# Carried state times C on two 64-row halves of the array, and y kept in two banks

## The chip, the core and the metric

The kernel runs on one core of a Trainium2 chip. The core has a matrix engine (TensorE, PE in the rows of the profile, with its weight loads shown apart as PEld), a vector engine (DVE), a scalar engine (ACT), a general engine (POOL) and a queue that only issues transfers (SP). They work side by side and wait for each other through semaphores. PE writes its products to PSUM, eight banks of 128 partitions by 2 KB; DVE and ACT read them from there into the on-chip memory SBUF. The metric is the device time of one execution in microseconds. Before the change it is 125.18 us, the median of three runs (125.15 to 126.35).

## What is computed

Two stages follow each other. The first is a state-space layer (4 batches, 8 heads, 768 tokens, 32 channels per head, state size 16), given in chunks; the second is a gated feed-forward layer on its output, 3072 tokens by 256.

```python
for c in range(nc):                       # chunks; state starts at zero
    cum = np.cumsum(la, axis=-1)          # la = log a, per batch and head
    M = einsum('bhin,bhjn->bhij', Cc, Bc) * exp(cum_i - cum_j) * causal
    y_intra = einsum('bhij,bhjd->bhid', M, xc)
    y_inter = einsum('bhin,bhnd->bhid', Cc, state) * exp(cum)
    y[:, :, sl] = y_intra + y_inter
    state = exp(sum(la)) * state + sum_j(Bc x xc * exp(cum_last - cum_j))
...
gate = maximum(x @ w_gate, 0); val = x @ w_val          # x = y, 3072 x 256
out = gate * val @ w_out                                # 256 -> 1536 -> 256
```

## The kernel before, in words

**Tiling.** The kernel takes chunks of 128 tokens, six to a batch, and handles them two at a time as a pair: p runs from 0 to 11, three pairs to a batch (`PPB` is 3). Pairs 0 to 5 (batches 0 and 1) load B and C by token and transpose them on PE. Pairs 6 to 11 (`p >= NRUN`, called packed in this text) take B and C from `seqB` and `seqC`, loaded once per batch in long runs along the sequence by `load_seq`, scaled on POOL (`seq_scale`), and turned by DVE (`seq_turn`, `seq_part`). The scale factors of these come from `ah`, the decays loaded by `load_a`.

**One pair.** `G` makes C times B for eight heads: 16 matmuls that use 32 rows and 128 columns of the array each (32\*128 in the profile), into four banks. `gevac` masks the products and brings them to `gs`, on ACT (then POOL for the mask) and on DVE. `Dm` and its inner `dterm` multiply them by x: 16 matmuls of 128 rows and 32 columns (128\*32) into y. `inter` adds the carried state times C to the same y. The states S come from `astep` and `sevac` (pairs 0 to 5), or from `arun` and its `evac` (packed pairs). `yevac` copies y to `yT`, the input of the feed-forward stage. Pairs 0 and 1 have `split_y` in place of `inter`, `Dm` and `yevac`; there y already has two banks, and the `dterm` matmuls come first.

**The carried state before.** For each chunk but the first of a batch, `inter` issues two matmuls with all 128 rows and columns (128\*128), one for each half t of the heads; the stationary operand is the masked state, 128 by 128, in which a row that belongs to the other half is zero. A pair so has four such matmuls (pairs 1, 2, 4, 5, 7, 8, 10, 11) or two (pairs 0, 3, 6, 9, whose first chunk has no carried state).

**Feed-forward.** It runs in blocks of 512 tokens, b from 0 to 5. `gv` and `gvp` make gate and val in two banks, ACT applies the relu to gate (`gv_relu`), DVE multiplies it by val (`gv_mul`). `fout` then makes the output in 12 matmuls per 128 tokens, ACT copies it (`foevac`), and SP or ACT sends it off.

**Order.** The order on every engine is the order in which the program is written: `in_order` chains the instructions. `section(p, n)` writes a pair's `inter` and `Dm`, the next pair's `arun` and `G`, and the evacuations; the last loop sets a block's `gv` calls, a section, two or three `outs`, another section and the last `outs` behind each other.

**Banks.** One of the eight PSUM banks holds the running state (`A_ps`). The other seven are handed out by `bank()` to whatever product comes next, each time one whose previous product has been read. A first matmul into a bank waits until the reader of the bank's previous product is through.

Of the kernel before, what the change touches and what calls it, by code (L numbers as in the profile page):

```python
# [29 lines left out]
def kernel(  # L30
# [43 lines left out]
    st = {}  # L74
# [91 lines left out]
    smasks = const.tile([128, 2, 2, 128], BF16)  # L166
# [138 lines left out]
    def load_a(q):  # L305
        q.dma_start(out=ah, in_=a[B0:NB].rearrange("b (t q) (j u) -> (q j) (b t) u", t=2, u=U))

    def seq_start():
        for v in (a0, tot, lead):
            nc.gpsimd.memset(v, 0.0 if v is a0 else 1.0)  # L310
        nc.gpsimd.memset(smasks, 0.0)
# [100 lines left out]
    def scale_bc(p, eng):  # L412
        b, c0 = p // PPB, 2 * (p % PPB)
        s = st[p]
        if p >= NRUN:
            bs = att.tile([128, 2, 128], BF16, tag="bt", name="bt")
            for t in range(2):
                hs = slice(4 * t, 4 * t + 4)
                eng.tensor_tensor(
                    out=bs.rearrange("s i (q t n) -> s i t q n", q=4, t=2)[:, :, t],  # L420
                    in0=s["br"][:, :, hs],
                    in1=scaleBC[:, b, c0:c0 + 2, 0, hs].unsqueeze(3).to_broadcast(
                        [128, 2, 4, N]), op=ALU.mult)
            s["B"] = [bs[:, i] for i in range(2)]
            return
# [174 lines left out]
    def arun(p):  # L600

        c0 = 2 * (p % PPB)
        for c in range(max(c0 - 2, 0), c0 + 1):
            v0, v1 = (0 if c < c0 else 1), (1 if c == c0 - 2 else 2)
            pc, i = p - (p % PPB) + c // 2, c % 2
            for q in range(4):
                out = XY[32 * q:32 * q + 32, v0:v1]
                rhs = st[pc]["x"][i].rearrange("s (t q d) -> s t q d", t=2, q=4)[:, :, q]
                nc.tensor.matmul(
                    out=out, lhsT=st[pc]["B"][i][:, 32 * q:32 * q + 32],  # L610
                    rhs=rhs.unsqueeze(1).to_broadcast([128, v1 - v0, 2, 32]),
# [3 lines left out]
        n = att.tile([128, 2, 2, 128], BF16, tag="SS", name="SS", bufs=3)  # L615

        def evac():
            shape = [128, 2 * (2 - v0), 4, 32]
            nc.vector.tensor_tensor(
                out=n[:, v0:2].rearrange("p v t (q d) -> p (v t) q d", q=4),  # L620
                in0=XY[:, v0:2].rearrange("p v (t d) -> p (v t) d", t=2).unsqueeze(
                    2).to_broadcast(shape),
                in1=smasks[:, v0:2].rearrange("p v t (q d) -> p (v t) q d", q=4),
                op=ALU.mult)
            for v in range(v0, 2):
                S[2 * p + v] = n[:, v]
# [3 lines left out]
    def y_bank(s):  # L630
        if "y" not in s:
            s["y"] = bank("y", (128, 2, 2, 128))
            s["open"] = False

    def split_y(p):

        s = st[p]
        yb = [bank("y%d" % k, (128, 2, 128)) for k in range(2)]
        carried = [S.pop(2 * p + i) if 2 * (p % PPB) + i else None for i in range(2)]
        for k in (1, 0):  # L640
            for i in range(2):
                dterm(p, yb[k][:, i], k, i, i == 0)
        for i in range(2):
            for k in (1, 0):
                if carried[i] is not None:
                    nc.tensor.matmul(
                        out=yb[k][:, i], lhsT=carried[i][:, k], rhs=s["CT"][:, i],
                        start=False, stop=True, skip_group_check=True)
        dst = yT[:, :, p * 256:(p + 1) * 256].rearrange("r t (i m) -> r t i m", i=2)
        nc.vector.tensor_copy(dst[:, 1], yb[1])  # L650
        nc.scalar.copy(out=dst[:, 0], in_=yb[0])

    def inter(p, i):
# [4 lines left out]
        Sm = S.pop(2 * p + i)  # L658
        for t in range(2):
            nc.tensor.matmul(  # L660
                out=s["y"][:, t, i], lhsT=Sm[:, t], rhs=s["CT"][:, i],
                start=not s["open"], stop=False, skip_group_check=True)
            s["open"] = True

    def dterm(p, out, k, i, start):

        s = st[p]
        for c in range(4):
# [3 lines left out]
                rhs=(s["gs"][:, c, 2 * i + k] if p >= NRUN else  # L672
                     s["gs"][:, h // 2, 2 * i + h % 2]), start=start, stop=True,
                tile_position=(0, 32 * c), skip_group_check=True)

    def Dm(p):
        s = st[p]
        y_bank(s)
        for i in range(2):
            for k in range(2):  # L680
                dterm(p, s["y"][:, k, i], k, i, not s["open"] and i == 0 and k == 0)
        s["open"] = True

    def yevac(p, eng):
        s = st[p]
        dst = yT[:, :, p * 256:(p + 1) * 256]
        src = s["y"].rearrange("r t i m -> r t (i m)")
        if eng is None:
            nc.scalar.copy(out=dst[:, 0], in_=src[:, 0])
            nc.vector.tensor_copy(dst[:, 1], src[:, 1])  # L690
        elif eng is nc.scalar:
            eng.copy(out=dst, in_=src)  # L692
        else:
            eng.tensor_copy(dst, src)
# [179 lines left out]
    dall = decay()  # L874
    decay_evac(dall)
# [44 lines left out]
    load_a(nc.scalar)  # L920
    gvp(0, 1, 2)
    gvp(0, 1, 4)
# [152 lines left out]
```

## Time and profile before

| | |
|---|---|
| median of the runs | 125.18 us (125.15 to 126.35) |
| the profiled execution's own time | 124.8 us |
| its span, from the first to the last instruction | 123.0 us |
| PE busy / its weight loads | 118.3 us (96%) / 81.1 us |
| DVE, ACT, POOL busy | 92.1, 74.6, 49.7 us |
| granted clock of PE, mean | 1.000 |

The profile's rows give a line of the kernel, the engine, the operation with output and inputs, its shape and how often it ran. In the list of groups busy time and the mean of one follow the bar, then the idle time ahead of them on their engine. In a timeline the row begins with its start and its length in us, and ends with the idle time of the engine before it and what ended that. A matmul's length includes its run through the array, so two that follow each other overlap in a timeline; the pitch from start to start tells what each costs PE.

### The profile page before, as it was taken

To read this page: it belongs to the slowest core of one execution; us is meant where nothing else is said; L and a number is where in the kernel's file an instruction comes from. 1 tells how busy PE (TensorE), PEld (TensorE's weight loads), DVE (VectorE), ACT (ScalarE), POOL (GpSimd) and SP (SyncE) were. 2 spreads that over 40 slices of the span, in tenths; PEclk is the share of its full clock that TensorE was granted. 3 is DMA by queue.
4 is the path that set the end of the run, shared out by engine and by line. 5 is a ranking of instruction groups with operands and counts; after the bars stand their busy time and mean duration, and the time that the engine had idled before them with its cause. 6 is when DMAs were issued, how large, how long until landed. Compare 5 with 4: busy or idle time off the path is not lost.

```text
span 123.0 us, 3313 instructions
## 1 busy us (share of the span) xinstructions
PE 118.3 (96%) x1251; PEld 81.1 (66%) x1257; DVE 92.1 (75%) x196; ACT 74.6 (61%) x148; POOL 49.7 (40%) x102
## 2 busy tenths in 40 slices
PE   6999999999999999999999999999999999999990
PEld 4678795578888989744478644588544587444780
DVE  2786898889999859879995889981898770678420
ACT  4376668888764461767663776746676644767310
POOL 7989741885745676477330640030700030000000
PEclk9999999999999999999999999999999999999999
DMA  2999999999989979969921282003200003100022
GB/s 61 201 193 209 168 167 190 130 102 174 162 101 278 140 137 191 199 201 211 132 24 62 83 137 22 5 0 106 70 3 0 0 5 128 43 0 0 0 91 85
DMA packets 63568, 12.95 MB, mean 105 GB/s; under 512 B 55168, under 2 KB 63552, under 8 KB 63552
## 3 DMA queue, kind: packets, MB, share of 16 engines
q1 hardware_dynamic: 54160, 9.47, 42.9%
q0 software_dynamic: 4272, 2.36, 14.6%
q10 hardware_dynamic: 5120, 0.90, 3.9%
q8 instruction: 10, 0.16, 0.5%
q14 instruction: 6, 0.05, 0.1%
HBM read 11.94 MB, written 3.15 MB: 123 GB/s over the span
## 4 chain that ended last, share of the span: by engine, by line
PE 95%; DVE 1%; issue 0%; ACTq 0%; ACT 0%; DVEq 0%
PE o L760 25%; PE val L707 20%; PE gate L704 18%; PE gate L734 7%; PE val L734 6%; PE w L189 4%; PE y L670 3%; PE g L544 3%; PE y L660 2%; PE A_ps L586 1%; PE tp L486 1%; PE wdec L232 1%; PE dec L279 1%; PE o L796 1%; PE bp L463 1%; PE fdec L247 0%
## 5 line engine op out<-in xcount | busy, mean ns | idle before, releaser
L719 DVE TENSOR_TENSOR h<-r,val 128x512 bf16<-128x512 bf16 x54 | 35.9, 685 | 10.2 <-ACT r L715 9.6
L715 ACT ACTIVATE r<-gate 128x512 bf16<-128x512 f32 x54 | 32.2, 598 | 12.2 <-PE gate L704 11.7
L707 PE MATMUL val<-yT,wv 128*128 128x512 bf16 x108 | 32.1, 379 | 0.3
L760 PE MATMUL o<-wo,h 128*128 128x256 bf16 x276 | 32.3, 273 | 0.0
L704 PE MATMUL gate<-yT,wg 128*128 128x512 bf16 x102 | 30.8, 379 | 0.0
L552 POOL TENSOR_SCALAR_AFFINE_SELECT gs<-gs 128x512 bf16<-128x512 bf16 (+1 forms) x26 | 13.6, 547 | 41.6 <-ACT gs L569 41.6
L760 PEld LDWEIGHTS <-h 128*128 128x128 bf16 x276 | 26.2, 98 | 4.0
L576 DVE TENSOR_TENSOR gs<-g,maskUT 128x512 bf16<-128x512 f32 (+1 forms) x32 | 17.6, 601 | 7.1 <-PE g L544 4.0
L707 PEld LDWEIGHTS <-wv 128*128 128x128 bf16 x108 | 10.6, 98 | 12.7
L704 PEld LDWEIGHTS <-wg 128*128 128x128 bf16 x108 | 10.4, 98 | 11.1
L569 ACT CAST gs<-g 128x512 bf16<-128x512 f32 (+1 forms) x26 | 11.8, 512 | 2.9 <-PE g L544 2.9
L742 ACT ACTIVATE r<-gate 128x512 bf16<-128x512 f32 x18 | 10.6, 604 | 2.7 <-PE gate L734 2.3
L749 DVE TENSOR_TENSOR h<-r,val 128x512 bf16<-128x512 bf16 x18 | 11.8, 678 | 0.3 <-ACT r L742 0.2
L734 PE MATMUL gate<-yT,wg 128*128 128x256 bf16 x72 | 10.8, 273 | 0.0
L734 PE MATMUL val<-yT,wv 128*128 128x256 bf16 x72 | 10.8, 273 | 0.0
L779 ACT COPY ob<-o 128x512 f32<-128x512 f32 x6 | 3.5, 586 | 8.6 <-PE o L760 8.6
L774 ACT COPY ob<-o 128x256 f32<-128x256 f32 x10 | 3.7, 373 | 7.3 <-PE o L760 6.8
L734 PEld LDWEIGHTS <-wv 128*128 128x128 bf16 x72 | 7.0, 98 | 0.9
L692 ACT CAST yT<-y 128x512 bf16<-128x512 f32 x10 | 5.9, 586 | 2.4 <-PE y L670 2.3
L734 PEld LDWEIGHTS <-wg 128*128 128x128 bf16 x72 | 6.7, 98 | 0.9
L189 PE MATMUL w<-warm 128*128 128x256 bf16 x27 | 5.9, 380 | 1.2 <-DVE tmask L159 1.2
L452 POOL CAST xb<-xr 128x512 bf16<-128x512 f32 x10 | 6.1, 612 | 1.0 <-DMA xr<-in_x_dram 1.0
(124 smaller groups left out, 123.2 us busy)
## 6 DMA issues: line engine op xcount, KB each, us to landing
xr<-in_x_dram SPq DMA_DIRECT2D x24, 128.0 KB, 3.7
out_dram<-ob SPq DMA_DIRECT2D x6, 256.0 KB, 2.6
out_dram<-ob SPq DMA_DIRECT2D x9, 128.0 KB, 1.8
wo<-in_moe_w_out_dram POOLq DMA_DIRECT2D x1, 768.0 KB, 8.9
seqB<-in_B_dram SPq DMA_DIRECT2D x2, 384.0 KB, 3.7
seqC<-in_C_dram SPq DMA_DIRECT2D x2, 384.0 KB, 4.2
br<-in_B_dram SPq DMA_DIRECT2D x12, 64.0 KB, 3.2
wg<-in_moe_w_gate_dram POOLq DMA_DIRECT2D x3, 128.0 KB, 4.3
```

What stands on the lines that cost most here:

```text
L189: nc.tensor.matmul(out=w[:, 0:cols], lhsT=warm[:, 0:128], rhs=warm[:, 0:cols], start=True, stop=True)
L552: nc.gpsimd.affine_select(out=dst, in_=dst, pattern=[[0, n], [1, 128]], compare_op=ALU.is_ge, fill=0.0, base=0, channel_multiplier=-1)
L569: nc.scalar.copy(out=d[:, q, h], in_=g[q][:, h])
L576: nc.vector.tensor_tensor(out=d[:, q, h], in0=g[q][:, h], in1=m[:, h], op=ALU.mult)
L704: nc.tensor.matmul(out=g, lhsT=wg[:, k, fs], rhs=yT[:, k, tk], start=(k == 0), stop=(k == 1))
L707: nc.tensor.matmul(out=v, lhsT=wv[:, k, fs], rhs=yT[:, k, tk], start=(k == 0), stop=(k == 1))
L715: nc.scalar.activation(r, g, AF.Relu)
L719: nc.vector.tensor_tensor(out=fst[b][:, f], in0=r, in1=v, op=ALU.mult)
L734: nc.tensor.matmul(out=o[:, j], lhsT=w[:, k, fs], rhs=yT[:, k, tk], start=(k == 0), stop=(k == 1), skip_group_check=True)
L742: nc.scalar.activation(r, g, AF.Relu)
L749: nc.vector.tensor_tensor(out=fst[b][:, f:f + 2, u * 256:(u + 1) * 256], in0=r, in1=v, op=ALU.mult)
L760: nc.tensor.matmul(out=o[:, ts % 2], lhsT=fst[b][:, f, ts * 128:(ts + 1) * 128], rhs=wo[:, f], start=(f == 0), stop=(f == NF - 1), skip_gr ...
```

## The change

- `inter` and `split_y` share a new function, `carried`. For each chunk it issues two matmuls that each use 64 rows and all 128 columns of the array: half k takes rows 64k to 64k+63 of the state and of C and writes y's half k. The number of matmuls stays as it was.
- y of a pair lies in two banks, `y0` and `y1`, one for each half, instead of one bank; `yevac` reads them with two copies.
- In packed pairs the heads stand in their natural order. `load_seq` and `load_a` fetch head 2q+t instead of 4t+q: four transfers where there were two, and four where there was one. Two of `load_a`'s transfers stand earlier, ahead of `decay_evac` on ACT; the other two stand behind `gvp(0, 1, 0)` and `gvp(0, 1, 2)`.
- The packed pairs' masked state has 128 columns per chunk instead of 256; `dmask` takes the place of `smasks`, filled by two POOL copies instead of a memset and eight. `scale_bc` of a packed pair is one POOL instruction instead of two.

```diff
@@ load_seq
-            q.dma_start(
-                out=r.rearrange("p t u n -> p t (u n)"),
-                in_=src[b].rearrange("(t q) (j u) n -> (q j) t (u n)", t=2, u=U))
+            for t in range(2):
+                q.dma_start(
+                    out=r[:, t].rearrange("p u n -> p (u n)"),
+                    in_=src[b].rearrange("(q t) (j u) n -> t q j (u n)", t=2, u=U)[t])
@@ load_a
-    def load_a(q):
-        q.dma_start(out=ah, in_=a[B0:NB].rearrange("b (t q) (j u) -> (q j) (b t) u", t=2, u=U))
+    def load_a(k):
+        nc.scalar.dma_start(
+            out=ah[:, k],
+            in_=a[B0 + k // 2].rearrange("(q t) (j u) -> t q j u", t=2, u=U)[k % 2])
@@ seq_masks
-        for q in range(4):
-            r = slice(32 * q, 32 * q + 32)
-            for v in range(2):
-                nc.gpsimd.tensor_copy(
-                    smasks[r, v, :, 32 * q:32 * q + 32],
-                    tmask[r].unsqueeze(2).to_broadcast([32, 2, 32]))
+        for k in range(2):
+            r = slice(64 * k, 64 * k + 64)
+            nc.gpsimd.tensor_copy(dmask[r].rearrange("p q m -> p (q m)"), smask[r, k])
@@ scale_bc
-            for t in range(2):
-                hs = slice(4 * t, 4 * t + 4)
-                eng.tensor_tensor(
...
+            eng.tensor_tensor(
+                out=bs.rearrange("s i (h n) -> s i h n", h=NH), in0=s["br"],
...
@@ arun
-                rhs = st[pc]["x"][i].rearrange("s (t q d) -> s t q d", t=2, q=4)[:, :, q]
+                rhs = st[pc]["x"][i][:, 64 * q:64 * q + 64]
...
-            shape = [128, 2 * (2 - v0), 4, 32]
+            shape = [128, 2 - v0, 2, 64]
...
@@ y_bank, carried
-            s["y"] = bank("y", (128, 2, 2, 128))
+            s["y"] = [bank("y%d" % k, (128, 2, 128)) for k in range(2)]
...
+    def carried(p, i, start):
+
+        s = st[p]
+        Sm = S.pop(2 * p + i)
+        for k in range(2):
+            r = slice(64 * k, 64 * k + 64)
+            nc.tensor.matmul(
+                out=s["y"][k][:, i], lhsT=Sm[r] if p >= NRUN else Sm[r, k],
+                rhs=s["CT"][r, i], start=start, stop=True, tile_position=(64 * k, 0),
+                skip_group_check=True)
@@ split_y
         for i in range(2):
-            for k in (1, 0):
-                if carried[i] is not None:
-                    nc.tensor.matmul(
-                        out=yb[k][:, i], lhsT=carried[i][:, k], rhs=s["CT"][:, i],
-                        start=False, stop=True, skip_group_check=True)
+            if 2 * (p % PPB) + i:
+                carried(p, i, False)
@@ inter
-        Sm = S.pop(2 * p + i)
-        for t in range(2):
-            nc.tensor.matmul(
-                out=s["y"][:, t, i], lhsT=Sm[:, t], rhs=s["CT"][:, i],
-                start=not s["open"], stop=False, skip_group_check=True)
-            s["open"] = True
+        carried(p, i, not s["open"])
+        s["open"] = True
@@ yevac
-        dst = yT[:, :, p * 256:(p + 1) * 256]
-        src = s["y"].rearrange("r t i m -> r t (i m)")
...
+        for k in range(2):
+            dst = yT[:, k, p * 256:(p + 1) * 256]
+            src = s["y"][k].rearrange("r i m -> r (i m)")
+            if eng is nc.scalar:
+                eng.copy(out=dst, in_=src)
...
@@ the program's order
     dall = decay()
+    load_a(0)
+    load_a(1)
     decay_evac(dall)
...
     gvp(0, 1, 0)
-    load_a(nc.scalar)
+    load_a(2)
     gvp(0, 1, 2)
+    load_a(3)
     gvp(0, 1, 4)
```

Line numbers of the two kernels differ a little: L660 and L646 (the carried matmuls) become L635, L670 (`dterm`) becomes L667, L760 (`fout`) becomes L754, L544 (`G`) becomes L540.

The first place is PE at pair 7, between the output matmuls of block 2 (`o`) and the `dterm` matmuls. `SS` is the masked state. Before:

```order
L760 MATMUL o_1463<-wo_146,h_1240 128x256
L660 LDWEIGHTS SS_1400
L660 MATMUL y_1479<-CTs_1114,SS_1400 128x128
...
L670 LDWEIGHTS xb_1253
L670 MATMUL y_1479<-gs_1421,xb_1253 32x128
```

After, at the same place:

```order
L754 MATMUL o_1470<-wo_146,h_1247 128x256
L635 LDWEIGHTS SS_1406
L635 MATMUL y0_1486<-CTs_1117,SS_1406 128x128
L635 LDWEIGHTS SS_1406
L635 MATMUL y1_1487<-CTs_1117,SS_1406 128x128
...
L667 LDWEIGHTS xb_1259
L667 MATMUL y0_1486<-gs_1427,xb_1259 32x128
```

There are four carried matmuls in both, each with its load of weights (the repeats are left out); they now go to the two banks in turn.

The second place is PE in block 3, where the last matmul of `G` is followed by the first output matmul of the block (`o`), with the semaphore that it waits for. Before:

```order
L544 MATMUL g2_1720<-CTs_1598,BM_1599 128x128
L544 LDWEIGHTS BM_1599
L544 MATMUL g3_1721<-CTs_1598,BM_1599 128x128
L760 LDWEIGHTS h_1565
L760 MATMUL o_1748<-wo_146,h_1565 128x256 [waits Activation_49]
```

After:

```order
L540 MATMUL g2_1728<-CTs_1606,BM_1607 128x128
L540 LDWEIGHTS BM_1607
L540 MATMUL g3_1729<-CTs_1606,BM_1607 128x128
L754 LDWEIGHTS h_1574
L754 MATMUL o_1757<-wo_146,h_1574 128x256 [waits DVE_49]
```

No instruction moved; the bank that `o` is given did. Before, it was that of the block's last `gate`, read by ACT. Now it is that of the last `val`, read by DVE's multiply. In block 4 it is the same; in block 2 `o` is given the bank that held y0 of the same section.

The third place is ACT early in the program, between the evacuation of pair 0's `G` and that of the decay products (`scaleBC`). Before:

```order
L569 CAST gs<-g_219 128x512
L569 CAST gs<-g_220 128x512
L289 COPY scaleBC<-dec 128x3x4x8 x2
L651 CAST yT<-y_278 128x256
L512 ACTIVATE BT<-tp,tmask 128x256
```

After:

```order
L565 CAST gs<-g_219 128x512
L565 CAST gs<-g_220 128x512
L307 DMA ah<-in_a_dram 128x1x24 x2
L290 COPY scaleBC<-dec 128x3x4x8 x2
L652 CAST yT<-y_280 128x256
```

Two transfers of `ah` are issued there now.

More of the change, by code (lines that the diff above doesn't have):

```diff
@@ L614, in arun @@
         v0 = 0 if c0 else 1
-        n = att.tile([128, 2, 2, 128], BF16, tag="SS", name="SS", bufs=3)
+        n = att.tile([128, 2, 128], BF16, tag="SS", name="SS", bufs=3)
         def evac():
-            shape = [128, 2 * (2 - v0), 4, 32]
+            shape = [128, 2 - v0, 2, 64]
             nc.vector.tensor_tensor(
[L620 to L624, printed above, removed]
+                out=n[:, v0:2].rearrange("p v (q m) -> p v q m", q=2),
+                in0=XY[:, v0:2].unsqueeze(2).to_broadcast(shape),
+                in1=dmask.unsqueeze(1).to_broadcast(shape), op=ALU.mult)
             for v in range(v0, 2):
@@ L680, in Dm @@
             for k in range(2):
-                dterm(p, s["y"][:, k, i], k, i, not s["open"] and i == 0 and k == 0)
+                dterm(p, s["y"][k][:, i], k, i, not s["open"] and i == 0)
         s["open"] = True
@@ L685, in yevac @@
         s = st[p]
[L686 to L694 removed]
+        for k in range(2):
[3 more added lines that the diff above has]
+                eng.copy(out=dst, in_=src)
+            else:
+                eng.tensor_copy(dst, src)
     fst = {}
```

23 lines of the change are left out of this document (9 added, 14 removed).

## The prediction

> **What bounds the kernel now.** I read the page first: the busy times and the chain that ended last, and then who waited for whom.
>
> ```profile
> span 123.0 us, 3313 instructions
> PE 118.3 (96%) x1251; PEld 81.1 (66%) x1257; DVE 92.1 (75%) x196; ACT 74.6 (61%) x148; POOL 49.7 (40%) x102
> ...
> PE 95%; DVE 1%; issue 0%; ACTq 0%; ACT 0%; DVEq 0%
> ```
>
> ```profile
> ACT r L715 <- PE gate L704: 11.7, 44, 0.3
> ```
>
> PE is busy for 118.3 of 123.0 us and carries 95% of the chain; ACT waits for PE 44 times, not the other way. So time is won or lost only where PE's pitch from start to start changes, or where PE comes to wait. The timeline of PE around pair 7 shows what a pair costs it:
>
> ```profile
> 66.69 0.39 PE L660 MATMUL y<-CTs,SS 128*128 128x128 bf16 x4
> 67.00 0.41 PE L670 MATMUL y<-gs,xb 128*32 128x128 bf16 x16
> 67.23 0.29 PE L609 MATMUL A_ps<-xb,bt 128*32 128x64 bf16 x12
> 67.45 0.40 PE L544 MATMUL g<-CTs,BM 32*128 32x128 bf16 x16
> 67.79 0.28 PE L760 MATMUL o<-wo,h 128*128 128x256 bf16 x1
> ```
>
> The list of groups gives one carried matmul 219 ns from entry to exit, and the number of them:
>
> ```profile
> L660 PE MATMUL y<-CTs,SS 128*128 128x128 bf16 x20 | 2.1, 219 | 0.0
> L660 PE MATMUL y<-CT,Sm 128*128 128x128 bf16 x14 | 1.4, 219 | 0.0
> L646 PE MATMUL y<-CT,Sm 128*128 128x128 bf16 x6 | 0.7, 222 | 0.0
> ```
>
> Four of them last 0.39 us together, so three pitches take 0.39 - 0.22 = 0.17 us: 0.057 us each. The 16 `dterm` matmuls use 32 columns each; they begin at 67.00, and L609, of the same shape, begins 0.23 later, which is four pitches of 0.057. So four matmuls in different strips of the array run at once. The 16 of L544, in four strips of rows, last 0.40 - 0.22 = 0.18 from first to last start, again about three pitches for sixteen. And a change of the array's shape costs: from the first carried matmul to the first `dterm` it is 0.31 us, but four pitches are 0.23; 0.08 is left. From L544's first to the output matmul it is 0.34, of which 0.23 are pitches; 0.11 is left. The count is right, too: 20 + 14 + 6 = 40 is eight pairs with four and four pairs with two.
>
> **The carried matmuls.** Two things change for each pair. Halves that run at once make four pitches into two (two into one). But `carried` has a shape of its own, 64 rows by 128 columns, that lies between the 128\*128 work before it and the 128\*32 of `dterm` behind it. Before, there was one change of shape here, 128\*128 to 128\*32; now there are two. In `split_y`, where `dterm` comes first and 128\*128 work behind, it is the same: one before, two now. The cost of going from 128\*128 to 64\*128 is in the trace, early on, where L586 is followed by L256; the same L586 followed by a matmul of its own shape stands a little later:
>
> ```profile
> 9.96 0.27 PE L586 MATMUL A_ps<-xb,bx 128*128 128x256 bf16 x1
> 10.16 0.38 PE L256 MATMUL fmid<-cp,sel 64*128 64x1 f32 x2
> ```
>
> ```profile
> 13.34 0.27 PE L586 MATMUL A_ps<-xb,bx 128*128 128x256 bf16 x1
> 13.45 0.27 PE L734 MATMUL gate<-yT,wg 128*128 128x256 bf16 x1
> ```
>
> 0.20 against 0.11: entering 64 rows costs 0.09. A pair with four matmuls so changes by 0.09 - 2 x 0.057 = -0.02, a pair with two by 0.09 - 0.057 = +0.03. Eight times -0.024 and four times +0.033 make -0.06 us. With the 0.08 and 0.11 above as the ends for the change of shape (12 x 0.08 or 12 x 0.11 against 20 pitches, 1.14 us) it is -0.18 to +0.18. I take -0.06: what the halves save, the extra change of shape takes back. That two halves do run side by side no row shows; the four strips of L544, each with its own bank, are nearest, and I take them.
>
> [...]
>
> **The banks.** y takes two of the seven shared banks, so from pair 2 on each product gets its bank one turn sooner. Going through the banks of both kernels, I find three places where a first matmul would now come before its bank is read: the first output matmul of blocks 2, 3 and 4 (the second place shown above). In time order, rows of the engines there:
>
> ```profile
> 62.41 0.59 ACT L692 CAST yT<-y 128x512 bf16<-128x512 f32 x1 [0.30 <-PE y L670]
> ...
> 62.74 4.10 PE L760 MATMUL o<-wo,h 128*128 128x256 bf16 x36
> ```
>
> ```profile
> 79.87 0.69 DVE L719 TENSOR_TENSOR h<-r,val 128x512 bf16<-128x512 bf16 x1 [0.17 <-ACT r L715]
> ...
> 80.49 1.16 PE L760 MATMUL o<-wo,h 128*128 128x256 bf16 x9
> ```
>
> ```profile
> 97.50 0.69 DVE L719 TENSOR_TENSOR h<-r,val 128x512 bf16<-128x512 bf16 x1 [0.18 <-ACT r L715]
> ...
> 98.21 0.94 PE L760 MATMUL o<-wo,h 128*128 128x256 bf16 x7
> ```
>
> PE starts about 0.05 after its releaser ends: POOL's scaling ends at 9.52 + 1.04 = 10.56, and the weight load that needs it begins at 10.61.
>
> ```profile
> 9.52 1.04 POOL L433 TENSOR_TENSOR bs<-bcr,wf 128x512 bf16<-128x512 f32 x1
> ...
> 10.61 0.10 PEld L486 LDWEIGHTS <-bs 128*128 128x128 bf16 x1
> ```
>
> Block 3: 79.87 + 0.69 + 0.05 = 80.61 against 80.49, a wait of 0.12. Block 4: 98.24 against 98.21, 0.03. Block 2: y0's copy is half of L692; a 256-wide copy on ACT is 0.36 long (below), so 62.41 + 0.36 + 0.05 = 62.82 against 62.74, 0.08 or a little less, since y0 is complete one round before y1. Together 0.2 us; from 0.1 (block 3 alone) to 0.3. No release elsewhere ends within 0.15 us of its new taker.
>
> **The copies of y.** Two copies of 256 take the place of one of 512, 0.59 long. ACT's pitch after a 256-wide copy is 11.64 - 11.39 = 0.25:
>
> ```profile
> 11.39 0.36 ACT L507 COPY CT<-tpc 128x256 bf16<-128x256 bf16 x1
> 11.64 0.61 ACT L742 ACTIVATE r<-gate 128x512 bf16<-128x512 f32 x1
> ```
>
> So y1 is through 0.25 + 0.36 = 0.61 after the start, 0.02 later than the one copy was; next on ACT stand the casts of `gs`, wanted only by the next pair's `dterm`. Nothing on PE; without that cover 0.02 a pair.
>
> **The early transfers of `ah`.** Two of four now stand ahead of `decay_evac`.
>
> ```profile
> 7.66 1.07 ACT L569 CAST gs<-g 128x512 bf16<-128x512 f32 x2 [0.22 <-PE g L544]
> 9.61 0.38 ACT L289 COPY scaleBC<-dec 128x96 f32<-128x96 f32 x2 [0.87 <-PE dec L279]
> ...
> 16.59 0.38 ACTq L306 DMA_DIRECT2D ah<-in_a_dram  x1
> ```
>
> An issue takes 0.38; two fit into the 0.87 that ACT idles before L289, which waits for PE. The other two issues lie where one lay, between relus that wait for PE. But the early ones add packets while pair 1's x is still on its way, and PE waits for that x:
>
> ```profile
> 14.15 0.40 ACT L455 CAST xb<-xr 128x256 bf16<-128x256 f32 x1 [0.53 <-DMA xr<-in_x_dram]
> ...
> 14.41 0.55 PE L670 MATMUL y<-gs,xb 128*32 128x128 bf16 x16
> ```
>
> ```profile
> q10 hardware_dynamic: 5120, 0.90, 3.9%
> ```
>
> L670 lasts 0.55 here and 0.41 at 67.00, so PE already loses 0.14 to this load: whatever delays it goes straight into the time. ACT's queue took 0.039 x 16 x 123.0 / 5120 = 0.015 us per packet; half of `ah` is 2 x 128 = 256 packets, 16 for each of the 16 transfer engines, 0.24 us. They may also land before x or behind it: 0 to 0.24, and I take 0.1. On SP, the two more issues of each `load_seq` push the loads behind them back:
>
> ```profile
> 40.30 0.58 SPq L106 DMA_DIRECT2D br<-in_B_dram  x1
> ```
>
> ```profile
> br<-in_B_dram SPq DMA_DIRECT2D x12, 64.0 KB, 3.2
> ```
>
> ```profile
> 46.89 0.76 POOL L419 TENSOR_TENSOR bt<-br,scaleBC 128x128 bf16<-128x128 f32 x2
> ```
>
> Pair 6's last load is issued by 40.88 and lands 3.2 later, at 44.1; two issues of 0.58 more make it 45.3, and POOL first reads it at 46.89. Nothing; without this cover 1.2 us, at one place in each batch.
>
> **Work off the path.** The mask of the packed states halves on DVE, and POOL's scaling needs one instruction instead of two:
>
> ```profile
> L619 DVE TENSOR_TENSOR SS<-A_ps,smasks 128x512 bf16<-128x512 f32 x4 | 2.7, 680 | 0.0
> L619 DVE TENSOR_TENSOR SS<-A_ps,smasks 128x256 bf16<-128x256 f32 x2 | 0.8, 414 | 0.0
> L419 POOL TENSOR_TENSOR bt<-br,scaleBC 128x128 bf16<-128x128 f32 x12 | 4.6, 405 | 0.0
> ```
>
> Four of 680 become 414-like, about 1.1 us of DVE; POOL loses six instructions. Neither engine ends a wait of PE there, so: nothing.
>
> **Sum.** -0.06 + 0.2 + 0.1 = +0.24 us. The profiled execution took 124.8 us, 1.8 more than its span, and lies 0.38 under the median of the runs. 124.8 + 0.24 + 0.38 = 125.4 us. A measurement of this kernel can tell about 1% from no change (its three runs already span that): below 123.9 is faster, above 126.4 slower.
>
> **Rivals.** First, the entry into 64 rows is free, because PE loads those weights while the 128\*128 work still runs. For it: nothing in the rows but that weight loads run ahead within one shape. Against: L256, and every other change of shape that I read. The pitches would be saved at no price: 125.4 - 12 x 0.09 = 124.3 us, which is not 1% either. Chance 0.13.
>
> Second, slower: the two halves do not overlap. The place is every `carried`; 20 pitches are then not saved and 12 entries are added: 12 x 0.09 = 1.08 instead of -0.06, so 126.5 us. It makes the kernel 1% slower from nine tenths of the pitches on; at half the overlap it is 126.0. For it: no row shows two strips of 64 rows together. Against: L544's and L670's strips of 32 do so in every pair. Chance 0.07.
>
> Third, the second chunk's weights, which go to the same rows as the first's, load only when those matmuls are through. A weight load of this size takes 98 ns:
>
> ```profile
> L660 PEld LDWEIGHTS <-SS 128*128 128x128 bf16 x20 | 1.6, 98 | 0.8
> ```
>
> Eight pairs with two rounds pay 0.1 each: 126.2 us. L544 speaks against it: its rounds use the same four strips of rows over and over at 0.057 or so. [...] Chance 0.05.
>
> Fourth, the early `ah` packets hold back one transfer engine, and x lands a microsecond late: 126.4 us or above. The x loads' worst landing is far above their median, which speaks for it:
>
> ```profile
> DMA to landing us min/median/max: 2.8/3.7/7.6
> ```
>
> Their small number, 16 an engine, speaks against it. Chance 0.04.
>
> **How the numbers follow.** The forecast has 0.66. Its low ends (-0.18, 0.1 and 0) give 124.8 + 0.38 - 0.08 = 125.1, its high ends (0.18, 0.3 and 0.24) 125.9. The range takes in the first and the third rival, 124.2 to 126.2; the second, the fourth and what I have not thought of (0.03 above, 0.02 below) stay out. Faster by over 1% needs more than the first rival gives, so it is the 0.02 of the unthought and a little of that rival's edge: 0.03. Slower by over 1% is the second and the fourth and part of the rest: 0.12. Within 1%: 0.85.
>
> **What would show it.** In the changed profile: the four carried matmuls should start in two rounds 0.057 apart, 0.09 later behind the output matmul than before, and the first `dterm` 0.2 after them. PE's first output matmul of block 3 should begin 0.05 after DVE's last multiply. L667 at about 14.4 should last 0.55 or more. The forecast is wrong if the entry takes less than 0.05, if the two halves start 0.05 apart, or if PE waits at a bank that I have not named.

## The result, and the profile after

The changed kernel takes 130.78 us (median of six runs, 129.09 to 133.51) against 125.17 us for the kernel before, measured beside it: a ratio of 1.038, with a 95% interval of 1.029 to 1.047. The forecast was 125.4 us, no change; by the two medians the kernel is slower by 5.6 us. The ratio leaves out the two of the six runs that lie over 1.5% above the fastest (131.19 and 133.51 us), so by it the loss is 4.8 us. The profiled execution took 130.76 us.

The page of the changed kernel, the rows that answer to those of before:

```profile
span 129.1 us, 3319 instructions
PE 119.6 (93%) x1251; PEld 79.6 (62%) x1257; DVE 89.5 (69%) x196; ACT 74.8 (58%) x158; POOL 47.3 (37%) x89
...
PE 49%; DMA 21%; SPq 16%; POOL 4%; ACT 4%; issue 2%; DVE 1%; ACTq 0%; POOLq 0%; DVEq 0%
```

PE is busy for 119.6 us, 1.3 more than before, but the span grew by 6.1. The chain, 95% PE before, now runs through transfers and SP's queue for more than a third. So PE waits, and the waits tell for what (engine and line, what it waited for, total, times, longest):

```profile
POOL pack L368 <- DMA seqB<-in_B_dram: 6.3, 2, 5.7
POOL pack L368 <- DMA seqC<-in_C_dram: 4.6, 2, 2.3
ACT ob L768 <- DMA out_dram<-ob: 4.5, 2, 3.5
POOL bt L416 <- DMA br<-in_B_dram: 4.3, 2, 3.9
...
PE y L667 <- POOL gs L548: 1.9, 1, 1.9
...
PE val L701 <- ACT ob L768: 1.3, 1, 1.3
```

In the kernel before, `pack` never waited for `seqB` or `seqC`, and ACT never for an output to leave. The loads named here are issued by SP, and so is the output for which ACT waits longest. Its timeline before, at an early issue and around the first `load_seq`:

```profile
27.14 4.16 SPq L115 DMA_DIRECT2D bcr<-in_B_dram  x1
...
36.30 0.47 SPq L129 DMA_DIRECT2D seqC<-in_C_dram  x1
36.86 0.41 SPq L105 DMA_DIRECT2D xr<-in_x_dram  x1
37.32 0.58 SPq L106 DMA_DIRECT2D br<-in_B_dram  x1
37.95 2.31 SPq L105 DMA_DIRECT2D xr<-in_x_dram  x1
```

and in the changed kernel:

```profile
36.02 1.42 SPq L130 DMA_DIRECT2D seqC<-in_C_dram  x2
37.54 0.94 SPq L105 DMA_DIRECT2D xr<-in_x_dram  x1
38.53 3.81 SPq L106 DMA_DIRECT2D br<-in_B_dram  x1
42.38 3.12 SPq L105 DMA_DIRECT2D xr<-in_x_dram  x1
45.55 0.58 SPq L106 DMA_DIRECT2D br<-in_B_dram  x1
```

Most issues of `br` take about 0.58 us. Here single ones take 3.81 and 3.12, where the longest before was 2.31. A long issue is nothing new (4.16 at 27.14 before); what is new is one at this place. SP hands over the loads of pair 6 only as the two tiles ahead of them go out: the last packet of the tiles starts at 45.15, and the next issue, at 45.55, takes 0.58 again. That is pair 6's last load; before it was issued at 40.30. The share of the sixteen DMA engines that is busy just then (the columns are the window, its length, busy us of each engine with the number of instructions, PE's clock, DMA share, GB/s), before:

```profile
core 0: us, PE busy (x) PEld busy (x) DVE busy (x) ACT busy (x) POOL busy (x), PEclk, DMA share, GB/s
37.00:39.00 2.00, 2.00 (x23) 1.79 (x21) 2.00 (x5) 1.12 (x3) 1.20 (x3) 1.00 0.94 253
```

and in the changed kernel, with a later window:

```profile
37.00:39.00 2.00, 2.00 (x22) 1.79 (x19) 1.88 (x3) 1.00 (x3) 1.38 (x2) 1.00 0.25 86
...
72.00:76.00 4.00, 3.78 (x17) 2.25 (x19) 1.95 (x4) 1.90 (x5) 3.27 (x6) 0.57 0.77 178
```

0.25 against 0.94, and 86 GB/s against 253: as much as a quarter of the engines would do, while the transfers behind wait. A sequence's two tiles are 512 packets of 1536 bytes in both kernels; from the first to the last start they take 3.0 us before and 9.0 (first load) and 9.6 (second) after. A single one of these packets takes 65 ns (median) in both. So not the packet is slower, but fewer are in flight: their times summed, over the time from the first start to the last end, make 13.0 before and 3.9 and 3.7 after.

PE's timeline has two stalls behind the first load,

```profile
49.97 0.21 PE L605 MATMUL A_ps<-xb,bt 128*32 128x64 bf16 x4 [0.33 <-POOL xb L448]
...
55.37 0.59 PE L701 MATMUL val<-yT,wv 128*128 128x512 bf16 x2 [1.27 <-ACT ob L768]
```

and the longest of all at the second:

```profile
68.67 0.29 PE L635 MATMUL y<-CTs,SS 64*128 64x128 bf16 x4
70.89 0.65 PE L667 MATMUL y<-gs,xb 128*32 128x128 bf16 x16 [1.94 <-POOL gs L548]
71.32 0.33 PE L605 MATMUL A_ps<-xb,bt 128*32 128x64 bf16 x12
```

And the chain that led to it:

```profile
58.81 9.65 DMA seqC<-in_C_dram
...
69.40 0.85 POOL pack L368
70.26 0.59 POOL gs L548
```

POOL works in order: `gs`, which PE wants, stands behind a `pack` that waits for its tile. From start to start of the matmuls, PE loses 0.50 us ahead of 49.97 (behind POOL's `xb`, which stands behind `pack` and `bt`), 1.44 ahead of 55.37 (behind ACT's `ob`, whose slot is still going out), 2.0 ahead of 70.89 and 0.20 behind it: 4.1 us. Then the clock drops: in the window from 72 to 76 it is 0.57, and 0.43 x 3.78 = 1.6 us go with it. That is 5.7 us of the 6.1 by which this execution's span is longer; some 0.4 is left for what the prediction had reckoned with. The drop of the clock is not the price of every execution: the granted clock was 0.987 in two of the six runs and 1.000 in four, and one of these took 130.81 us. Where that run lost the time is not on record.

### The profile page after: what moved, and what is told of

It is laid out like the page before. It is cut to its first block, busy times and chain, and to the rows that moved or that the text cites. A ratio compares the mean times of both kernels' runs of the same rounds, so it can differ in the third digit from the quotient of the medians.

```text
span 129.1 us, 3319 instructions
## 1 busy us (share of the span) xinstructions
PE 119.6 (93%) x1251; PEld 79.6 (62%) x1257; DVE 89.5 (69%) x196; ACT 74.8 (58%) x158; POOL 47.3 (37%) x89
## 4 chain that ended last, share of the span: by engine, by line
PE 49%; DMA 21%; SPq 16%; POOL 4%; ACT 4%; issue 2%; DVE 1%; ACTq 0%; POOLq 0%; DVEq 0%
PE o L754 13%; PE gate L698 13%; PE val L701 11%; DMA seqC<-in_C_dram 7%; SPq L115 6%; DMA bcr<-in_C_dram 5%; DMA out_dram<-ob 4%; SPq L113 3%; SPq L106 3%; DMA ah<-in_a_dram 3%; SPq L105 2%; ACT r L709 2%; PE gate L728 2%; PE y L667 2%; DMA br<-in_B_dram 2%
## 5 line engine op out<-in xcount | busy, mean ns | idle before, releaser
L754 PE MATMUL o<-wo,h 128*128 128x256 bf16 x276 | 33.1, 277 | 0.1
L701 PE MATMUL val<-yT,wv 128*128 128x512 bf16 x104 | 31.5, 381 | 1.4 <-ACT ob L768 1.3
L698 PE MATMUL gate<-yT,wg 128*128 128x512 bf16 x106 | 32.2, 385 | 0.5 <-ACT r L709 0.2
L754 PEld LDWEIGHTS <-h 128*128 128x128 bf16 x276 | 26.7, 99 | 4.3
L728 PE MATMUL gate<-yT,wg 128*128 128x256 bf16 x72 | 10.8, 273 | 0.0
L728 PE MATMUL val<-yT,wv 128*128 128x256 bf16 x72 | 10.8, 273 | 0.0
L686 ACT CAST yT<-y 128x256 bf16<-128x256 f32 x20 | 6.5, 376 | 4.2 <-PE y L667 4.0
L667 PE MATMUL y<-gs,xb 128*32 128x128 bf16 x192 | 5.1, 222 | 2.0 <-POOL gs L548 1.9
```

The source lines that it names most:

```text
L698: nc.tensor.matmul(out=g, lhsT=wg[:, k, fs], rhs=yT[:, k, tk], start=(k == 0), stop=(k == 1))
L701: nc.tensor.matmul(out=v, lhsT=wv[:, k, fs], rhs=yT[:, k, tk], start=(k == 0), stop=(k == 1))
L728: nc.tensor.matmul(out=o[:, j], lhsT=w[:, k, fs], rhs=yT[:, k, tk], start=(k == 0), stop=(k == 1), skip_group_check=True)
L754: nc.tensor.matmul(out=o[:, ts % 2], lhsT=fst[b][:, f, ts * 128:(ts + 1) * 128], rhs=wo[:, f], start=(f == 0), stop=(f == NF - 1), skip_gr ...
```

## The experiments

**Theory 1:** the new form of the sequence loads is served by few DMA engines. In `load_seq` the rows of the DRAM side now step by head 2q+t; for one t these are 4 blocks (q) of 32 rows, which do not merge, so the transfer's DRAM side begins with a dimension of 4. Before, head group and segment merged to 128. **Theory 2:** the number of transfers on SP, which doubled, pushes all behind it back. **Theory 3:** the loss is PE's own, by bank waits and changes of shape. **Theory 4:** the transfers of `ah` are what clogs. The first four kernels tell them apart.

**The load by pairs of heads.** Four transfers a tile, each with 32 segments as its leading dimension:

```diff
-            for t in range(2):
-                q.dma_start(out=r[:, t].rearrange("p u n -> p (u n)"),
-                    in_=src[b].rearrange("(q t) (j u) n -> t q j (u n)", t=2, u=U)[t])
+            for h in range(4):
+                q.dma_start(out=r[32 * h:32 * h + 32].rearrange("p t u n -> p t (u n)"),
+                    in_=src[b, 2 * h:2 * h + 2].rearrange("t (j u) n -> j t (u n)", u=U))
```

> The changed kernel, but each sequence tile (seqB, seqC) is loaded by four transfers of 32 partitions x 2 heads of the pair, instead of two transfers of 128 partitions x 1 head of each pair: the same bytes to the same places, twice as many transfers as in the change, eight a sequence. Theory 1 (a transfer whose DRAM side begins with a dimension of 4 is served by only few of the 16 DMA engines, and holds up what is queued behind it): the loss goes, 125.0 to 126.2 us; the packets of a load take about 3 to 4 us again instead of 9, pack no longer waits 5.7 us, and the output slots are free in time. Theory 2 (more DMA instructions on SyncE push the later loads back): worse than the change, 131 us or more, since there are eight where there were four. Theory 3 (TensorE: the bank waits and the changes of array shape): stays at 130.8.

125.08 us, a ratio of 1.0027 (0.9995 to 1.0058). With twice as many transfers as the change has, the loss is gone, and 10.8 and 9.2 packets are in flight. Theories 2 and 3 fall.

**Two transfers a tile in the kernel before, in the old order.**

```diff
-            q.dma_start(
-                out=r.rearrange("p t u n -> p t (u n)"),
-                in_=src[b].rearrange("(t q) (j u) n -> (q j) t (u n)", t=2, u=U))
+            for t in range(2):
+                q.dma_start(out=r[:, t].rearrange("p u n -> p (u n)"),
+                    in_=src[b].rearrange("(t q) (j u) n -> t (q j) (u n)", t=2, u=U)[t])
```

> The kernel before, with only the sequence loads split into two transfers a tile as in the change, but in the old order of the heads, in which head group and segment merge into one dimension of 128 on the DRAM side. Theory 1 (few DMA engines): nothing is lost, 125.2 us within 0.4. Theory 2 (the number of transfers on SyncE): most of the loss appears, 128 to 131 us. Theory 3 (TensorE): 125.2.

124.83 us, 1.0004 (0.9972 to 1.0036): splitting by itself costs nothing that can be measured.

**The change's load alone, in the kernel before.** The diff of `load_seq` from the change, and nothing else.

> The kernel before, with only the sequence loads of the change: two transfers a tile in the natural order of the heads, 4 x 32 x 384 elements on the DRAM side. The consumers still take the old order, so the heads of batches 2 and 3 are computed with each other's B and C; the instructions and the bytes are the same, and the time stands for the load alone. Theory 1 (few DMA engines): nearly the whole loss appears, 129 to 131.5 us, with pack waiting some 5 us on seqB and TensorE at half clock after its longest stall. Theory 2: the same 129 to 131. Theory 3 (TensorE) and theory 4 (the four transfers of the decay tile ah): 125.2.

130.11 us, 1.040 (1.032 to 1.049): the whole loss, with the carried matmuls, the banks and `ah` as they were. PE's timeline shows the same stall in front of the same matmuls, here at the first load:

```profile
48.60 0.39 PE L661 MATMUL y<-CT,Sm 128*128 128x128 bf16 x4
51.19 0.65 PE L671 MATMUL y<-gs,xb 128*32 128x128 bf16 x16 [2.20 <-POOL gs L553]
```

**`ah` by pairs of heads as well.** The load by pairs of heads, and

```diff
-    def load_a(k):
-        nc.scalar.dma_start(out=ah[:, k],
-            in_=a[B0 + k // 2].rearrange("(q t) (j u) -> t q j u", t=2, u=U)[k % 2])
+    def load_a(k):
+        r = slice(32 * k, 32 * k + 32)
+        for i in range(NB - B0):
+            nc.scalar.dma_start(out=ah[r, 2 * i:2 * i + 2],
+                in_=a[B0 + i, 2 * k:2 * k + 2].rearrange("t (j u) -> j t u", u=U))
```

> As the first of these kernels, and the decay tile ah is loaded by eight transfers of 32 partitions (one for each pair of heads and batch; the first four early, the rest late), instead of four of 128 partitions with a leading dimension of 4 on the DRAM side. Theory 1: the loss was in the sequence loads, so this is within 0.4 us of the first kernel, 125.0 to 126.2. Theory 4 (ah's transfers on few engines, early in the kernel, start the delay): the first kernel stays at 128 or more and this one comes to 125.

125.37 us, 1.0039 (1.0000 to 1.0077), the same as without it. Theory 4 falls.

**The dose.** If the leading dimension sets the number of engines, other sizes must give other times. In the kernel before, the rows of a tile were taken as 8 x 16 and as 2 x 64:

```diff
+                    in_=src[b].rearrange("h (t j u) n -> t h j (u n)", t=2, u=U)[t])
...
+                    in_=src[b].rearrange("(g t h) (j u) n -> t g (h j) (u n)", t=2, g=2, u=U)[t])
```

> The kernel before, with each sequence tile loaded by two transfers whose DRAM side begins with a dimension of 8 (8 heads x 16 segments) instead of 4; rows come to other partitions than the reference wants, so batches 2 and 3 are computed from mixed-up B and C, with the same instructions and bytes. Theory 1 (the leading dimension sets how many of the 16 engines serve a transfer): eight engines instead of four, so the load's packets take about half of the 9.0 us that they took in the change, some 4.5 us against 3.0 in the kernel before; pack begins 2.6 us after the last packet in the kernel before, so most of it is hidden: 124.7 to 126.2 us. If only the number of dimensions of the transfer counted, or that it doesn't merge: as with 4, 129 to 131.

> As the run with a leading dimension of 8, but with one of 2 (2 x 64 rows); batches 2 and 3 are again computed from mixed-up B and C. Theory 1: two engines, so the load's packets take about 18 us a sequence, pack waits some 13 us twice where it waited 5: 138 to 150 us. If only the unmerged transfer counted: 129 to 131.

124.98 us, 1.0031 (1.0008 to 1.0054), and 147.27 us, 1.181 (1.177 to 1.184). The window from 37 to 39 with a leading dimension of 8:

```profile
37.00:39.00 2.00, 2.00 (x20) 1.80 (x19) 1.88 (x3) 0.97 (x2) 1.35 (x2) 1.00 0.44 131
```

and with 2, with its longest wait of PE:

```profile
PE y L671 <- POOL gs L553: 15.7, 2, 7.9
```

```profile
37.00:39.00 2.00, 2.00 (x21) 1.79 (x19) 1.88 (x3) 0.97 (x2) 1.10 (x2) 1.00 0.15 23
```

| leading dimension (kernel) | DMA share, 37 to 39 us | packets of first / second load, us from first to last start | ratio |
|---|---|---|---|
| 128 (before) | 0.94 | 3.0 / 3.0 | 1 |
| 128, two transfers a tile | 0.95 | 3.7 / 3.5 | 1.0004 |
| 32 (by pairs of heads) | 0.87 | 3.9 / 4.7 | 1.0027 |
| 8 | 0.44 | 6.9 / 6.0 | 1.0031 |
| 4 (the change) | 0.25 | 9.0 / 9.6 | 1.038 |
| 2 | 0.15 | 17.2 / 17.1 | 1.181 |

4 of 16 is 0.25, 2 of 16 is 0.13, 8 of 16 is 0.50: the share is close to the leading dimension over sixteen, other transfers included. The packets in flight, worked out as above, follow it too: 6.6 and 6.9 at 8, 3.9 and 3.7 at 4, 2.1 at 2, with 65 ns for a packet in every run. The load's length was expected at 4.5 us for 8 and came out at 6 to 7; going from 4 to 2 about doubles it (9.0 and 9.6 to 17.2 and 17.1). The trace has no row for each engine, so which ones were busy is not shown. At 8 the loads take twice as long as before and the kernel loses only 0.3%: `pack` waits 4.0 us for `seqB` there, once, but no wait of PE comes of it.

**One load at a time.** Each of these has the change's form in one of the two loads and four transfers a tile in the other; the second of them has `b != B0` in the first line.

```diff
+            if b == B0:
+                for h in range(4):
...
+                continue
```

> The changed kernel with the first sequence (batch 2) loaded by eight transfers of 32 partitions and the second (batch 3) left as in the change. Theory: the loss of 5.6 us lies in two places. The stalls of TensorE at 49 to 54 us (0.49 and 1.44) go with the first load, the stall at 68.8 (2.0 us, with some 2 us at half clock behind it) stays with the second: 128.5 to 130 us. Rival (the first load's delay is passed on, and all that comes later is its result): 125 to 126.

124.65 us, 0.9997 (0.9982 to 1.0011). My theory of two places was wrong, the rival right: with the first load in order, the second may be as slow as in the change. POOL waits for it about as long as in the changed kernel,

```profile
POOL pack L375 <- DMA seqB<-in_B_dram: 5.2, 1, 5.2
...
POOL pack L375 <- DMA seqC<-in_C_dram: 2.3, 1, 2.3
```

but no stall of PE comes of it: SP issues it at 52.6 instead of 57.05, early enough.

> The reverse of the run in which only the first sequence load was mended: the first sequence (batch 2) is loaded as in the change, by two transfers a tile with a leading dimension of 4, and the second (batch 3) by eight transfers of 32 partitions. Mending the first alone took the whole loss away. If the first load's delay costs only what its own waits show (0.49 + 1.44 us at 49 to 54) and the rest came of the second load being issued 4.6 us late and then lasting 9.5 us, this is 126.8 to 127.8 us; if the second load's late issue alone did it, whatever its length, 129.5 to 131.

128.62 us, 1.031 (1.028 to 1.034). This lies between the two ranges: the first load alone costs 3.9 us, more than the 2 that its waits in the changed kernel came to. Two more stalls of PE follow, this time behind DVE:

```profile
64.43 0.59 PE L708 MATMUL val<-yT,wv 128*128 128x512 bf16 x2 [0.99 <-DVE h L720]
...
66.22 0.40 PE L547 MATMUL g<-CTs,BM 32*128 32x128 bf16 x14 [0.35 <-DVE h L720]
```

DVE's late mask work (`CTs` and `BM`, for the first sequence) now falls together with POOL's `pack` for the second, in this timeline of DVE and that of POOL:

```profile
62.02 1.76 DVE L404 TENSOR_SCALAR BM<-seqTB,words 128x120 uint32<-128x120 uint32 x2
```

```profile
61.12 1.70 POOL L375 TENSOR_TENSOR pack<-seqB,hd 128x384 bf16<-128x384 f32 x2 [2.14 <-DMA seqB<-in_B_dram]
62.78 1.72 POOL L375 TENSOR_TENSOR pack<-seqC,hd 128x384 bf16<-128x384 f32 x2
```

With only the first load in order, the same two instructions ran while POOL was idle, and took 0.55:

```profile
58.23 0.55 DVE L404 TENSOR_SCALAR BM<-seqTB,words 128x120 uint32<-128x120 uint32 x2
```

So DVE comes late to `h`, which PE waits for, and delays do not add up by place: a late first load also sets when the second is issued, and what runs beside what.

**Whose wait it is.** In the changed kernel both `pack` and the loads behind the sequence are late. Here pair 6's loads go first:

```diff
-    load_seq(2, nc.sync)
     load(6, nc.sync)
+    load_seq(2, nc.sync)
```

> The changed kernel with the loads of pair 6 issued ahead of the first sequence load instead of behind it, all on SyncE; the sequence loads themselves are left as in the change. If what the first load held up is pair 6's x and B, queued behind it: their wait (4.3 us on GpSimd) goes and the time falls to 126 to 128 us. If it is pack's own wait for seqB and seqC, or the later loads and the outputs behind the sequence on the queue: no better, 130 to 132.

131.1 us, 1.050 (1.047 to 1.053): no better. The waits say why:

```profile
POOL pack L368 <- DMA seqB<-in_B_dram: 5.7, 1, 5.7
...
PE y L667 <- POOL gs L548: 3.5, 1, 3.5
...
POOL bt L416 <- DMA br<-in_B_dram: 0.9, 1, 0.9
```

POOL's waits for B fall from 4.3 to 0.9, but the sequence starts later (its first packet at 39.78 instead of 36.18) and PE waits 3.5 us behind `pack`. The expectation had put the 4.3 us down to pair 6. By POOL's order they belong to pairs 7 (0.40) and 8 (3.91); the `bt` of pair 6 waited for no load in the changed kernel, it stood behind `pack`. So this run could not win what was expected of it. Reordering moves the delay; it does not take it away.

**Another queue.**

```diff
-    load_seq(2, nc.sync)
+    load_seq(2, nc.scalar)
...
-            load_seq(3, nc.sync)
+            load_seq(3, nc.scalar)
```

> The changed kernel with both sequence loads issued by ScalarE at the same place of the program instead of by SyncE; still two transfers a tile with a leading dimension of 4. Theory 1a (what is queued behind them on SyncE's queue is held up): the output slots and the loads of x and B come in time, the stalls at 49 to 54 go, while pack still waits for its own tile: about 127 to 129 us. Theory 1b (the few engines that serve them are shared whatever the queue, and pack's own wait decides): 129.5 to 131.

133.02 us, 1.068 (1.065 to 1.071): neither. On ACT nothing held the first load back, so that it went out at 14.9 us and not at 35, among the first x loads. ACT's timeline and the wait that it made:

```profile
14.90 0.55 ACTq L130 DMA_DIRECT2D seqB<-in_B_dram  x1
...
18.20 2.20 ACTq L307 DMA_DIRECT2D ah<-in_a_dram  x1
```

```profile
POOL xb L448 <- DMA xr<-in_x_dram: 6.8, 1, 6.8
```

The x that is late here was issued by SP (at 24.33, where the kernel before has it at 18.35), the slow load by ACT: another queue did not keep SP's loads clear of it. ACT's own work suffers as well. Its relu of a gate began only at 20.50, when the issue of `ah` (18.20 to 20.40), stuck behind the slow load, was through, and PE waited for that:

```profile
21.15 0.27 PE L482 MATMUL tpc<-ident,bs 128*128 128x128 bf16 x2 [1.33 <-ACT r L736]
```

How much each of the two costs, and what the same move would do at the old time, is not shown: ACT and SP reach that place 20 us apart.

**The banks alone,** in the kernel before:

```diff
-            s["y"] = bank("y", (128, 2, 2, 128))
+            s["y"] = [bank("y%d" % k, (128, 2, 128)) for k in range(2)]
...
-                out=s["y"][:, t, i], lhsT=Sm[:, t], rhs=s["CT"][:, i],
+                out=s["y"][t][:, i], lhsT=Sm[:, t], rhs=s["CT"][:, i],
```

> The kernel before with y alone changed: two banks and two copies a pair, in the old order of the heads and with the carried matmuls over 128 rows. The prediction's term for the banks: three waits of TensorE, 0.2 us together (0.1 to 0.3), so a ratio of about 1.0016 and waits at the first output matmul of blocks 2, 3 and 4. If the banks cost nothing: 1.000.

1.0013 (0.9994 to 1.0031), 0.16 us: the size predicted, though the interval takes in none at all. Its profiled execution (125.12 us) does not have the three waits as predicted. Block 3 has 0.12 and block 4 has 0.03; in block 2 the output matmul does not wait, but PE waits ahead of it, inside `G`, behind DVE's `h`; `G` uses nothing that `h` makes, so what it waits for can only be the bank that `h` reads:

```profile
62.62 0.40 PE L544 MATMUL g<-CTs,BM 32*128 32x128 bf16 x14 [0.31 <-DVE h L717]
```

That is a wait at a bank that the prediction had not named, one of its signs of being wrong. DVE is late there: the two instructions of its `BM` took 1.75 us beside POOL's `pack`. In the kernel before they took 1.15, and PE did not wait.

**The carried matmuls alone.** The kernel with only the first load in order, with 128 rows again:

```diff
-        n = att.tile([128, 2, 128], BF16, tag="SS", name="SS", bufs=3)
+        n = att.tile([128, 2, 2, 128], BF16, tag="SS", name="SS", bufs=3)
...
-                out=s["y"][k][:, i], lhsT=Sm[r] if p >= NRUN else Sm[r, k],
-                rhs=s["CT"][r, i], start=start, stop=True, tile_position=(64 * k, 0),
+                out=s["y"][k][:, i], lhsT=Sm[:, k],
+                rhs=s["CT"][:, i], start=start, stop=True,
```

> The kernel with only the first sequence load mended (ratio 0.9997), in which the carried matmuls go back to 128 rows and the packed states to 256 columns with the other half zero; natural order and two banks stay. It isolates the carried matmuls. The prediction's term: the halves change the time by -0.06 us (-0.18 to +0.18), so this one is within 0.2 us of the mended kernel, a ratio of 0.998 to 1.001. If entering 64 rows were free, this one would be 1.1 us longer, 1.009; if the halves did not overlap, 1.1 us shorter, 0.991.

124.32 us, 0.9979 (0.9966 to 0.9991): the fastest of all, by 0.3 us against the kernel before. The halves cost by that 0.9997 - 0.9979 = 0.0018, about 0.2 us, with intervals that overlap. PE's timeline around a pair with two carried matmuls, with halves:

```profile
84.32 0.23 PE L642 MATMUL y<-CTs,SS 64*128 64x128 bf16 x2
84.48 0.41 PE L674 MATMUL y<-gs,xb 128*32 128x128 bf16 x16
```

and with all rows:

```profile
84.01 0.28 PE L641 MATMUL y<-CTs,SS 128*128 128x128 bf16 x2
84.22 0.41 PE L673 MATMUL y<-gs,xb 128*32 128x128 bf16 x16
```

0.16 from the first of them to `dterm` against 0.21: the halves save 0.05 here. But the output matmul before them starts 0.205 ahead with halves, 0.109 without. By the start times of all twelve pairs, from the matmul before to the one behind: seven pairs with four gain 0.005 each, three with two lose 0.051 each, and `split_y` loses 0.041 in pair 0 and 0.039 in pair 1. Together +0.20 us, as the runs have it. (In pair 1 the four matmuls of this kernel stand 0.066 to 0.080 apart, those of the kernel before 0.056 to 0.065; against the latter the halves lose 0.075 there.) Why this kernel also beats the one before with two banks alone (1.0013), from which it differs by the order of the heads, its loads and the work off the path, was not tried further.

## Why the prediction was wrong

**The step that failed** is the one on SP: "Pair 6's last load is issued by 40.88 and lands 3.2 later, at 44.1; two issues of 0.58 more make it 45.3, and POOL first reads it at 46.89. Nothing". It priced the new transfers by their count. What changed was their form: the same bytes went out with 3.9 packets in flight instead of 13, and the kernel before with nothing but that load showed the whole loss (1.040). Pair 6's last load was issued by 46.13 and not by 42.0, and POOL, which had its own tile to wait for first, began `bt` late:

```profile
45.93 1.67 POOL L368 TENSOR_TENSOR pack<-seqC,hd 128x384 bf16<-128x384 f32 x2 [2.30 <-DMA seqC<-in_C_dram]
...
48.74 0.62 POOL L416 TENSOR_TENSOR bt<-br,scaleBC 128x256 bf16<-128x256 f32 x1 [0.20 <-issue]
```

48.74 against 46.89. The step named its cover (1.6 us from 45.3 to 46.89) and a price without it, "1.2 us, at one place in each batch"; the delay was 5.2 us for the first load (45.15 against 39.95 for the start of its last packet), and the price 4.8 to 5.6 in all. It also looked only at the loads behind; `pack`, which reads the tiles themselves, was not in it. In the kernel before, `pack` began 2.0 us behind the last packet of the two tiles (39.95 to 41.97), two fifths of the delay.

**The carried matmuls.** Predicted -0.06 us (-0.18 to +0.18); measured about +0.2. The mechanism was right: the halves start 3 to 4 ns apart in the changed kernel, so that they do run side by side, and the extra change of shape takes back what they save: entering 64 rows costs 0.096 (0.205 against 0.109, 0.312 against 0.216), where the step said 0.09. Two sizes were off. The second round starts 0.067 behind the first and not 0.057, and a single round leaves 0.157 to `dterm`, not 0.149. And in `split_y`, called "the same: one before, two now", the way back from 64 rows to 128 costs 0.159 where 128 to 128 took 0.056. A pair with four so gains 0.005, not 0.02, and one with two loses 0.05, not 0.03. The first rival (entry free) and the second (no overlap) are both ruled out by these numbers, the third by the rounds 0.067 apart.

**The banks.** Predicted waits at the first output matmul of blocks 2, 3 and 4: 0.08, 0.12, 0.03. Measured from the last matmul of `G` to the output matmul, 0.183, 0.270 and 0.186 against 0.147 everywhere else: 0.04, 0.12, 0.04. The sum, 0.2 us, is as predicted; block 2 has half of its share. In block 3 of the changed kernel:

```profile
85.96 0.40 PE L540 MATMUL g<-CTs,BM 32*128 32x128 bf16 x16
86.42 4.09 PE L754 MATMUL o<-wo,h 128*128 128x256 bf16 x36
```

0.46 from start to start; blocks 2 and 4 have 0.37, the places without a wait 0.33 or 0.34. The wait inside `G` that the kernel with the two banks alone showed is not in this list.

**`ah`, the copies, DVE and POOL.** Pair 1's x was not held back: L667 at 14.42 took 0.41 and not "0.55 or more", 0.14 less than before. The 0.1 taken for `ah` and the fourth rival did not come about. The two copies of y took 0.65 together (0.61 predicted), and no wait came of it. DVE has 2.6 us less to do (the step said 1.1) and POOL 2.4, and neither showed in the time.

**The sum.** With the load in order, the rest of the change measures +0.33 us (ratio 1.0027) or -0.04 (0.9997, the second load left slow), where the terms said +0.24 and the corrected ones say +0.4. Both lie inside the range of 124.2 to 126.2, so the forecast would have stood without the one step. Slower by over 1% had a chance of 0.12, put on PE's shape and on x; none of it was for the reason that came true.

## What to carry to other kernels

When a transfer's pattern changes, compare the dimensions of its DRAM side and not its bytes or its count: ask whether what had merged into one large leading dimension still does, and if not, split the transfer so that each part leads with a large one, as the four transfers of 32 segments did here (3.9 and 4.7 us a load; 8 already took 6.9 and 6.0, twice the 3.0 of 128). Then follow both the reader of the tile and everything behind it on the same queue, since on engines that work in order one late tile holds back work that has nothing to do with it (here `gs` behind `pack`, 2.0 us of PE). Packing matmuls into halves of the array just broke even at four in a row here, since a change of the array's shape cost 0.096 us, as much as the two pitches saved (from the first of the four to the last it was 0.168 before and 0.070 after).

## What the runs showed of the hardware

- A transfer's leading dimension of 2, 4 and 8 kept the busy share of the DMA engines at 0.15, 0.25 and 0.44 where 128 gave 0.94, and 2.1, 3.9 and 6.6 packets in flight where 128 gave 13.0, at 65 ns a packet throughout. The queue behind it went on only as it drained: single issues on SP took 3.81 us.
- PE's clock fell to half (0.50 from 73 to 75) after a pause of 1.94 us, some 1.5 us after PE was back, and stayed so for 3.4 us (0.57 on average from 72 to 76, so 4 x 0.43 / 0.5); after the pauses of 1.27 in the changed kernel and of 1.04 and 0.99 with the second load in order it stayed at 1.00. Around the pause of 1.94, PE was busy for 0.11 of the 2 us from 69 to 71. With the loads on ACT the clock fell at 21.60, 0.45 us after a pause of 1.33 had ended and within the next, of 0.45. What decides on the drop is not shown.
- Two of DVE's mask instructions (128x120 uint32) took 1.76 us beside POOL's `pack` (1.75 in the kernel with the two banks alone) and 0.55 without it; in the kernel before, where they overlapped in part, 1.15.
